# Half-size products for a third chunk of the first MLP matrix, with sums on GpSimd, finer waits and more filler matmuls

## The chip, the cores and the metric

The kernel runs on one core of a Trainium2 chip. The metric is the device time of one execution in microseconds (us). Three executions of the kernel before took 300.26, 300.62 and 301.41 us; the median is 300.62. The engines are TensorE (PE in the profile, with its weight loads as PEld), VectorE (DVE), ScalarE (ACT), GpSimd (POOL) and SyncE (SP).

## The reference

Eight batches, eight heads, 576 positions, head size 64. Attention looks back over a window of 128 positions with a linear bias per head; its output is laid side by side by heads to rows of 512, and goes through a normalisation, a two-layer MLP (512 to 2048 to 512) and a residual add.

```python
mask = (rel >= 0) & (rel < window)
scores = np.where(mask, scale * q @ k.T + slopes * -abs(rel), -1e9)
attn = softmax(scores)                      # by row
x = (attn @ v).transpose(0, 2, 1, 3).reshape(B, S, H * D)     # 8 x 576 x 512
xn = (x - mean) / sqrt(var + 1e-6) * g_ln
out = x + np.maximum(xn @ w_ch1, 0.0) @ w_ch2
```

## The kernel before

The 4608 rows are 36 blocks of 128. Blocks are gathered into 11 chunks: four of 2 blocks (chunks 0 to 3) and seven of 4 blocks (chunks 4 to 10). A program that ran before the kernel was written down has fixed the order of all work: the text `ORDER` (line 119) is a list of words `name:engine`, where `T` is TensorE (with the PSUM bank as a number), `V` VectorE, `A` ScalarE, `G` GpSimd and `S` SyncE. A word `~n` stands for n filler matmuls of 128x128 that compute nothing (`keep_warm`, L1287). Each engine runs its own words in the order of the list, and waits only for the data and buffers that a task needs. Tasks are declared with the engines they may run on and a planner's cost in us; the cost doesn't appear in the built program.

Per block: q and k come in by GpSimd DMA issues (L496) with a cast to f16, from block 9 on a SyncE DMA turns them (`QT`, L710, into `qkt`); before that TensorE does (`T`, L695). `S` multiplies k by q into the PSUM tiles `sc` (L732); ScalarE takes the exponential into `probs` (`exa`, `exb`, L780); from block 5 on VectorE multiplies `probs` by a table (`mka`, `mkb`, L787), of which there are three kinds: `mreg`, `mmix` and `mnew`. `pva` and `pvb` multiply by v (L808); VectorE normalises (`rc`, `nm`, L825 and L829) into `xb`, takes mean and variance (`bn`, `ag`), and writes `xs` (L892), which a SyncE DMA turns into `xt` (`XT`, L921).

Per chunk: the first MLP product is 16 tasks `A` of four matmuls 128x512 (L1210), each with a relu into `ht` (`r`, L1225 and L1227). The second product of chunks 0 to 3 is plain (`B`, L1247). From chunk 4 on it is made as seven half-size products instead of eight (`seven`, tasks `Pa` to `Pg`, L992), after the scheme of Strassen and Winograd: sums `sa` to `sd` of quarters of `ht` (two halves each, L982) and sums of the weights made once (`sumT`, L952), and reads of PSUM with adds (`ra` to `rg`, L1004).

In the last two chunks (`BOTH = 9`, chunks 9 and 10) the first product is made in the same way (`fours`): for each of four groups of outputs, seven products `Ua` to `Ug` of four matmuls 128x256 (L1121) with sums of the weights (`sumW`, made once in `first_sums`, L1079) and sums of `xt` (`tx`, L1098), copies of products out of PSUM (`ca`, `cb`, `cc`, L1132 and L1134), adds `ja` to `jc` (L1144) and relus (`rja` to `rjd`, L1149, L1151, L1180).

Sums lie in buffers that their owners no longer need: `sumW` in the three tables, `tx` in tiles of the `qkt` ring, the copies in tiles of the `probs` ring. Before the change all of them wait for the last mask product, and for the last reader of all tiles of `probs` and `qkt` (the list `free` in `first_sums`). All sums are VectorE's. The four PSUM banks `u` of the first product take the place of `sc` when the first `Ua` comes.

Of the kernel before, what the change touches and what calls it, by code (L numbers as in the profile page):

```python
# [119 lines left out]
dist:G qs0.0.i:S iden1:G ks0.0.i:S dist01:G dist00:G qs1.0.i:S iden2:G sid5:V sid3:V ks1.0.i:S sid2:V sid0:V sid1:V sid4:V sid7:V sid6:V v0.i:S  # L120
iden3:V ~38 Za0:T0 Zb0:T0 cT0.00:A g.i:A cT0.10:G w0.i:G ~16 T0.0:T0 cT0.01:A q2.i:G eT0.00:V cT0.11:V k2.i:G ~8 Sa0:T0 T0.1:T1 exa0:A v1.i:G eT0.01:A
eT0.10:V Za1:T0 cv0:A G:T2 q3.i:G eT0.11:A k3.i:G Sb0:T0 Gc:A Sa1:T0 exb0:A pva0:T0 v2.i:G Gk:T1 rc0.0:V exa1:A nm0.0:V Zb1:T0 w3.i:G pvb0:T2 Sb1:T0
rc1.0:V nm1.0:V v3.i:G exb1:A mu0:V xs0:V w1.i:G ~10 T2:T0 Z2:T0 w2.i:G ev2:V pvb1:T2 pva1:T3 q5.i:G rc1.1:V S2:T0 rc0.1:V nm1.1:V TX0:T0 exb2:A
nm0.1:V q4.i:G xt0:V exa2:A ~4 T3:T2 mu1:V k4.i:G xs1:V Z3:T0 ev3:A bn1:V w4.i:G TX1:T3 pva2:T0 pvb2:T2 xt1:V S3:T0 Gkc:V rc0.2:V w5.i:G rc1.2:V
A0.0:T3 nm0.2:V exb3:A nm1.2:V w6.i:G A0.12:T1 mu2:V exa3:A xs2:V A0.14:T0 bn0:V r0.12:A r0.0:V pvb3:T2 r0.14:A Z4:T0 rc1.3:V ag0:V pva3:T1 w7.i:G
nm1.3:V A0.2:T3 rc0.3:V nm0.3:V TX2:T0 mu3:V A0.6:T2 xs3:V xt2:A A0.4:T1 r0.6:V k5.i:G bn3:V TX3:T0 r0.4:A A0.8:T2 v4.i:G bn2:V xt3:A ag1:V A0.10:T1
ag2:V k6.i:G r0.8:A A1.14:T0 q6.i:G r0.10:V r0.2:V A1.12:T2 r1.14:A ln0:A T4:T1 rs0:A r1.12:A A1.0:T3 ev4:A q7.i:G A1.4:T0 B1.0:T2 r1.4:V r1.0:V
A1.6:T1 k8.i:G S4:T0 A1.10:T0 exa4:A r1.6:A B0.0:T3 r1.10:A k8.i:G exb4:A B1.4:T2 A1.2:T1 sumT0.0:V B0.4:T3 r1.2:V q8.i:G B1.8:T2 sumT0.1:V k7.i:G
sumT0.2:V B0.8:T3 q8.i:G sumT0.3:V B1.12:T2 q9.i:G T5:T0 o1.0:V B0.12:T3 ev5:A v5.i:G sumT1.0:V pvb4:T1 B2.0:T2 o0.0:V k9.i:G mreg30:A mreg10:A
rc1.4:V mreg11:A pva4:T0 nm1.4:V S5:T0 mreg01:A k10.i:G rc0.4:V nm0.4:V B3.0:T3 exb5:A sumT1.1:V v6.i:G T6:T1 mu4:V exa5:A ag3:V xs4:V q10.i:G A1.8:T0  # L130
ev6:V mreg20:A B3.4:T3 k11.i:G mreg31:A bn4:V mreg21:A ln1:A S6:T0 mreg00:A r1.8:V v7.i:G rs1:A T8:T1 mkb5:V exb6:A dist2:G T7:T0 ev8:V B3.8:T3
q11.i:G exa6:A mka5:V pvb5:T1 q12.i:G ev7:V B2.4:T2 rc1.5:V QT9.i:S nm1.5:V v8.i:G pva5:T0 B2.8:T2 rc0.5:V nm0.5:V k12.i:G mka6:V S7:T0 v8.i:G mu5:V
B2.12:T2 mkb6:V exb7:A QT10.i:S xs5:V v9.i:G TX4:T1 exa7:A B3.12:T3 xt4:V k13.i:G mmixc:V TX5:T0 pva6:T1 o3.0:V xt5:A S8:T0 q13.i:G o2.0:V pvb6:T0
exb8:A A2.2:T3 v11.i:G mkb7:V A2.8:T2 mnewc:V r2.2:A v10.i:G QT11.i:S z2:V mka7:V A2.0:T3 r2.8:A rc1.6:V rc0.6:V z1:V A2.14:T2 r2.0:A nm1.6:V mkb8:V
exa8:A A2.12:T0 nm0.6:V sumT1.2:V pvb7:T3 r2.12:A pva7:T1 bn5:V S9:T0 r2.14:A QT12.i:S rc1.7:V A2.4:T0 z3:V exb9:A ag4:V nm1.7:V A2.10:T2 mu6:V exa9:A
xs6:V A2.6:T3 k15.i:G rc0.7:V bn6:V XT6.i:S r2.4:A mka8:V S10:T0 q15.i:G r2.6:A nm0.7:V B5.0:T0 r2.10:A mu7:V exa10:A ag6:V xs7:V pvb8:T3 pva8:T1
B5.4:T0 ag5:V exb10:A bn7:V XT7.i:S k16.i:G rc1.8:V B4.0:T2 mka9:V k15.i:G nm1.8:V QT13.i:S S11:T0 rc0.8:V dist2a:G nm0.8:V q15.i:G B4.4:T2 mkb9:V
exb11:A v13.i:G bn8:V B5.8:T0 exa11:A mkb11:V q14.i:G pvb9:T3 pva9:T1 ln2:A mka11:V B4.8:T2 rs2:A k14.i:G ag8:V rc0.9:V rc1.9:V B5.12:T0 nm0.9:V
v12.i:G ag7:V nm1.9:V ln3:A B4.12:T2 rs3:A bn9:V k17.i:G mkb10:V pvb11:T1 A3.2:T3 q16.i:G ag9:V o4.0:V ln9:A rs9:A S12:T0 r3.2:A q17.i:G xs8:V
rc1.11:V pva11:T2 o5.0:V XT8.i:S exb12:A A3.0:T3 xs9:V exa12:A A3.4:T0 nm1.11:V XT9.i:S rc0.11:V mka10:V A3.8:T1 r3.4:A nm0.11:V bn11:V A3.6:T0 r3.8:A  # L140
mkb12:V r3.0:A pvb10:T2 pva10:T1 QT14.i:S rc1.10:V S13:T0 rc0.10:V nm0.10:V A3.10:T3 exa13:A nm1.10:V out1.0.i:S bn10:V pvb12:T1 out0.0.i:S r3.6:A
A3.14:T2 ag11:V r3.10:V B6.0:T0 ag10:V r3.14:V ln11:A rs11:A exb13:A A3.12:T3 xs10:V mka13:V XT10.i:S scaleW2:A B7.0:T2 xs11:V r3.12:V B6.4:T0
XT11.i:S scaleW3:V B7.4:T2 scaleW1:A QT15.i:S B6.8:T0 rc1.12:V mkb13:V nm1.12:V B7.8:T2 k19.i:G B6.12:T0 QT16.i:S scaleW0:A v15.i:G S14:T0 o6.0:V
v14.i:G pva13:T3 mka12:V B7.12:T2 out2.0.i:S rc0.13:V exa14:A nm0.13:V pvb13:T1 pva12:T0 o7.0:V A4.8:T3 v20.i:G exb14:A rc1.13:V rc0.12:V nm1.13:V
A4.1:T2 v16.i:G nm0.12:V QT17.i:S mkb14:V S15:T0 r4.1:A v15.i:G mka14:V A4.3:T1 exb15:A bn12:V q18.i:G A4.0:T0 sumT1.3:V exa15:A k18.i:G r4.8:V
A4.10:T2 mka15:V q21.i:G S16:T0 r4.10:A r4.3:V A4.12:T3 q19.i:G exb16:A r4.0:V A4.11:T2 bn13:V q20.i:G exa16:A ag12:V r4.12:V A4.4:T1 dist1:G r4.11:A
mkb15:V k20.i:G A4.9:T0 r4.4:A ag13:V mka16:V v17.i:G ln13:A pvb14:T3 rs13:A A4.15:T2 r4.9:A xs12:V rc1.14:V XT12.i:S nm1.14:V pva14:T1 pva15:T0
rc0.14:V A4.7:T3 nm0.14:V QT18.i:S rc0.15:V nm0.15:V A4.14:T1 r4.7:A xs13:V mkb16:V A4.2:T0 out3.0.i:S bn14:V pvb15:T3 r4.2:A S17:T0 r4.15:A sa4.0:V
A4.6:T0 r4.14:A rc1.15:V sb4.0:V exb17:A A4.5:T2 XT13.i:S nm1.15:V r4.6:A A4.13:T1 bn15:V out6.0.i:S r4.5:A ag14:V sc4.0:V Pa4.00:T3 r4.13:A Pb4.00:T0
QT19.i:S exa17:A sa4.1:V Pa4.01:T3 Pb4.01:T0 ag15:V ln15:A Pa4.10:T3 out5.0.i:S rs15:A Pb4.10:T0 xs14:V out4.0.i:S Pa4.11:T3 xs15:V XT14.i:S Pb4.11:T0  # L150
sb4.1:V pvb16:T2 ra4.0:V k23.i:G pva16:T1 S18:T0 XT15.i:S rb4.0:V k21.i:G Pc4.00:T3 exb18:A Pc4.10:T3 sd4.0:V Pd4.00:T0 v24.i:G rc1.16:V exa18:A
QT20.i:S mka17:V Pc4.11:T3 Pd4.01:T0 k22.i:G rc0.16:V nm1.16:V Pc4.01:T3 mkb17:V Pd4.10:T0 v19.i:G rc4.0:V pva17:T2 Pd4.11:T0 q22.i:G nm0.16:V S19:T0
rd4.0:V Pe4.00:T3 v18.i:G exb19:A sc4.1:V Pe4.10:T3 pvb17:T1 rc0.17:V dist1a:G Pf4.10:T0 q23.i:G rc1.17:V nm0.17:V Pf4.00:T0 sd4.1:V Pe4.11:T3 q24.i:G
Pe4.01:T3 nm1.17:V Pf4.11:T0 k22.i:G QT21.i:S Pf4.01:T0 A5.0:T2 q22.i:G rf4.0:V A5.9:T1 bn17:V v23.i:G r5.0:A re4.0:V exa19:A A5.7:T0 v22.i:G mkb19:V
Pg4.00:T3 q25.i:G r5.9:V S20:T0 bn16:V Pg4.10:T3 k24.i:G exa20:A mka19:V A5.2:T2 v21.i:G mkb18:V Pg4.11:T3 QT23.i:S r5.2:A r5.7:V Pg4.01:T3 k25.i:G
# [58 lines left out]
def kernel(  # L214
# [49 lines left out]
    HALVED = []  # L264
    SPANS = [0]
    SEVEN = 4
    BOTH = 9
    BEFORE = 28.0
    AHEAD = 1.2
    SUMS_V = 40.0  # L270
# [700 lines left out]
    def seven(c, relu, v0):  # L971
# [8 lines left out]
        def sums(name, h, out, in0, in1, op, deps, v):  # L980
            def emit(e, b):
                nc.vector.tensor_tensor(out=out, in0=in0, in1=in1, op=op)  # L982
# [347 lines left out]
```

## Time and profile before

| | |
|---|---|
| median of three executions | 300.62 us |
| the profiled execution | 300.98 us, span of the instructions 299.1 us |
| TensorE busy | 293.3 us, 3014 matmuls, mean granted clock 0.994 |
| VectorE busy | 242.8 us |
| ScalarE busy | 165.3 us |
| GpSimd busy | 105.4 us, DMA issues nearly all |
| first product of the first chunk starts | 19.6 us |
| last matmul starts | 295.6 us |

Matmuls are pipelined, and the profile models their ends, so a busy TensorE may still lose time between two starts. A wait of an engine is put down to the last thing that released it. GpSimd's DMA issues count as busy time of GpSimd.

### The profile page before, as it was taken

Reading aid. Unit: us, or ns where it says so; the run is one execution under the profiler, and the core shown is the slowest. Engines: PE = TensorE matmul, PEld = TensorE weight load, DVE = VectorE, ACT = ScalarE, POOL = GpSimd, SP = SyncE. Lnnn points to the kernel's source line nnn. Section 1 sums busy time; section 2 is a strip of 40 time slices with the busy share of each in tenths; the row PEclk is TensorE's granted clock in tenths of the full one; section 3 lists DMA queues with packets and bytes.
Section 4 is the critical chain, followed back from the end, with each engine's and each line's share of the span. In section 5 each row is a group of like instructions: output and inputs, shape, how many; then the busy total and the mean of one; then the engine's idle time right before and its main releaser. Section 6 shows DMA issues by size and latency. Waiting matters only on the chain.

```text
span 299.1 us, 7458 instructions
## 1 busy us (share of the span) xinstructions
PE 293.3 (98%) x3014; PEld 225.1 (75%) x3014; DVE 242.8 (81%) x583; ACT 165.3 (55%) x273; POOL 105.4 (35%) x138
## 2 busy tenths in 40 slices
PE   8999999999999999899999999999999999999995
PEld 8789756875955578566886588657787799999984
DVE  3397289998879879849978888788899988988983
ACT  3664536794798573368528444676544655245500
POOL 5965369738137428433633567300000000000000
PEclk9799999999999999999999999999999999999999
DMA  6999999999999999999999999968101033012015
GB/s 179 159 196 194 206 144 141 146 138 133 122 219 145 151 224 133 145 140 167 179 166 197 182 159 143 158 171 150 36 19 55 0 125 89 2 37 106 35 55 193
DMA packets 163779, 39.93 MB, mean 133 GB/s; under 512 B 154017, under 2 KB 159137, under 8 KB 163746
## 3 DMA queue, kind: packets, MB, share of 16 engines
q0 software_dynamic: 110000, 17.70, 95.6%
q1 hardware_dynamic: 53744, 21.77, 40.5%
q8 instruction: 23, 0.38, 0.6%
q14 instruction: 10, 0.08, 0.1%
q10 hardware_dynamic: 2, 0.00, 0.0%
HBM read 36.70 MB, written 9.44 MB: 154 GB/s over the span
## 4 chain that ended last, share of the span: by engine, by line
PE 94%; DMA 4%; DVE 1%; ACT 0%; issue 0%
PE fb L1210 32%; PE fb L992 27%; PE fb L1247 9%; PE u L1121 8%; PE sc L732 6%; PE fb L808 6%; DMA qkt<-qk 4%; PE fb L1287 2%; PE sc L748 1%; PE fb L695 1%; PE fb L440 0%; PE fb L906 0%; PE fb L426 0%; DVE ot L1004 0%; DVE xb L829 0%; ACT probs L780 0%
## 5 line engine op out<-in xcount | busy, mean ns | idle before, releaser
L1210 PE MATMUL fb<-xt,w1sb 128*128 128x512 f16 (+1 forms) x576 | 106.4, 332 | 0.6 <-DMA xt<-xs 0.6
L780 ACT ACTIVATE probs<-sc 128x1024 f16<-128x1024 f32 (+1 forms) x72 | 67.4, 975 | 36.0 <-PE sc L732 27.3
L1210 PEld LDWEIGHTS <-w1sb 128*128 128x128 f16 x576 | 61.5, 114 | 27.8 <-DMA xt<-xs 0.9
L1227 ACT ACTIVATE ht<-fb 128x512 f16<-128x512 f32 x88 | 51.1, 598 | 44.4 <-PE fb L1210 44.2
L992 PEld LDWEIGHTS <-ht 128*128 128x128 f16 x560 | 53.2, 98 | 9.2
L496 POOL DMA_DIRECT2D qk<-in_k_dram x38 | 32.8, 866 | 44.3 <-DMA qkt<-qk 36.8
L992 PE MATMUL fb<-w2sb,ht 128*128 128x256 f16 x336 | 44.7, 273 | 0.0
L496 POOL DMA_DIRECT2D qk<-in_q_dram x38 | 32.5, 861 | 16.6 <-DMA qkt<-qk 9.6
L496 POOL DMA_DIRECT2D vx<-in_v_dram x36 | 31.0, 868 | 15.6 <-PE fb L808 12.4
L787 DVE TENSOR_TENSOR probs<-probs,mreg 128x1024 f16<-128x1024 f16 (+1 forms) x46 | 30.4, 667 | 1.1 <-ACT probs L780 1.0
L992 PE MATMUL fb<-ks,ht 128*128 128x256 f16 x224 | 30.8, 273 | 0.0
L1247 PE MATMUL fb<-w2sb,ht 128*128 128x512 f16 x128 | 30.7, 379 | 0.0
L829 DVE SCALAR_TENSOR_TENSOR xb<-fb,rec 128x256 f16<-128x256 f32 x72 | 29.5, 416 | 0.9
L808 PEld LDWEIGHTS <-probs 128*128 128x128 f16 x544 | 23.9, 98 | 6.8
L808 PE MATMUL fb<-vx,probs 128*128 128x65 f16 x496 | 26.1, 194 | 0.0
L1004 DVE TENSOR_TENSOR ot<-fb,xb 128x512 f32<-128x512 f32 (+1 forms) x31 | 19.6, 634 | 6.0 <-PE fb L992 5.6
L848 DVE BATCH_NORM_STATS2 st<-xb 128x6 f32<-128x512 f16 x36 | 24.2, 682 | 0.2
L825 DVE RECIPROCAL rec<-fb 128x4 f32<-128x4 f32 x72 | 12.2, 174 | 14.7 <-PE fb L808 12.4
L1225 DVE TENSOR_SCALAR ht<-fb 128x512 f16<-128x512 f32 x24 | 16.0, 681 | 8.4 <-PE fb L1210 8.3
L1247 PEld LDWEIGHTS <-ht 128*128 128x128 f16 x128 | 11.6, 98 | 11.1
L732 PEld LDWEIGHTS <-qkt 64*128 64x128 f16 x496 | 14.9, 94 | 6.4 <-issue 5.3
L1144 DVE TENSOR_TENSOR ht<-u,probs 128x512 f16<-128x512 f32 x24 | 16.2, 685 | 2.7 <-PE u L1121 1.8
(113 smaller groups left out, 387.7 us busy)
## 6 DMA issues: line engine op xcount, KB each, us to landing
out_dram<-ot SPq DMA_DIRECT2D x32, 256.0 KB, 2.9
qk<-in_q_dram POOLq DMA_DIRECT2D x30, 128.0 KB, 7.6
qk<-in_k_dram POOLq DMA_DIRECT2D x30, 128.0 KB, 7.2
vx<-in_v_dram POOLq DMA_DIRECT2D x28, 128.0 KB, 7.7
w1sb<-in_moe_w_ch_dram POOLq DMA_DIRECT2D x4, 512.0 KB, 9.1
w2sb<-in_moe_w_ch_dram POOLq DMA_DIRECT2D x4, 512.0 KB, 14.1
out_dram<-ot SPq DMA_DIRECT2D x8, 128.0 KB, 1.8
qs<-in_q_dram SPq DMA_DIRECT2D x2, 256.0 KB, 3.6
```

The lines of the kernel that those rows point to most:

```text
L496: nc.gpsimd.dma_start(out=dst(p0, n), in_=src[b, :, s0 : s0 + n, :].rearrange("h p d -> p h d"))
L732: nc.tensor.matmul(scs[half][:, g, c0 : c0 + P], kt[rows, 1, hp, :], qkt[i][rows, 0, hp, :], start=not bias, stop=True, skip_group_check=True,
L780: nc.scalar.activation(out=o, in_=n_, func=AF.Exp, scale=inv_sqrt_d)
L787: en.tensor_tensor(out=pv, in0=pv, in1=mask[:, 2 * half : 2 * half + 2, :, lo:], op=ALU.mult)
L808: nc.tensor.matmul(pp[:, hh * (D + 1) : hh * (D + 1) + D + 1], probs[i][:, bank, slot, side * P : side * P + P], vx[i if side else before] ...
L829: nc.vector.scalar_tensor_tensor(out=xb[c][:, j, 256 * half : 256 * half + 256].rearrange("p (h d) -> p h d", d=D), in0=pp[:, :, 0:D], sca ...
L848: nc.vector.bn_stats(out=st[i][:, :], in_=xb[c][:, j, :])
L992: nc.tensor.matmul(o, lhs(f, p), rhs(f), start=first and f == 0 and (p == 0 or key[0] != key[1]), stop=f == F2 - 1, skip_group_check=True)
L1121: nc.tensor.matmul(late[bank][:, FOURTH * f : FOURTH * f + FOURTH], w, rhs[kb], start=first and f == kb == 0, stop=kb == 1, skip_group_che ...
L1210: nc.tensor.matmul(fb[b][:, n_ * x : n_ * x + n_], w1f[f // CB][:, kb, (f + x) % CB, :], xt[c][:, kb, 0:n_], start=(kb == x == 0), stop=(k ...
L1227: nc.scalar.activation(out=o, in_=src, func=AF.Relu)
L1247: nc.tensor.matmul(pm[:, 0 : c1 - c0], ht[c][:, f, j * P : j * P + P], w2sb[f // CB][:, f % CB, c0:c1], start=(f == 0), stop=(f == NFB - 1),)
```

## The change

1. `BOTH` goes from 9 to 8: chunk 8's first product is made with seven half-size products for each of four groups, too.
2. The sums that lie in SBUF alone (`sa` to `sd`, `sumW`, `tx`) may run on GpSimd. In the new order 31 of the 56 `sa` to `sd`, all 8 `sumW` and 8 of now 12 `tx` do.
3. The waits are finer: a `sumW` waits for the masks that use its table alone, a `tx` for the readers of its tile of `qkt`, a copy for the readers of its tile of `probs`, and the first `Ua` for the exponentials, whose PSUM banks it takes. The three `sumW` buffers are dealt to the tables in another order.
4. The whole list `ORDER` is new. Its opening has fillers `~38 ~23 ~15 ~6 ~6 ~7` where it had `~38 ~16 ~8 ~10 ~4`; some tasks of the opening have changed engines, the loads of weights and of q, k and v stand in another order, and so do the transposes on SyncE.

Pieces of the order after the change, the first from the opening, the second from chunk 8 and 9:

```
sid4:V ~38 Za0:T0 cT0.00:A Zb0:T0 g.i:A cT0.10:G w0.i:G ~23 T0.0:T0 cT0.01:V q2.i:G eT0.00:A cT0.11:V k2.i:G eT0.01:V ~15 Sa0:T0 T0.1:T1 exa0:A v1.i:G
eT0.10:V ~6 Za1:T0 eT0.11:V Sb0:T0 cv0:G G:T2 exb0:A q3.i:G k3.i:G Zb1:T0 Gc:V pva0:T0 Sa1:T0 rc0.0:V v2.i:G pvb0:T1 nm0.0:V Sb1:T0 exa1:A rc1.0:V
...
sa8.0:G rjc8.2:A Ug8.3:T0 Uc9.0:T0 jc8.3:V rjd8.3:A Ud9.0:T0 bn35:V cb9.0:A Ua9.1:T0 ra8.0:V Pb8.01:T3 ca9.1:A sb8.0:G Ub9.1:T0 cc9.0:V rjc8.3:A
Pb8.10:T3 rjb8.2:A ja9.1:V Ue9.0:T0 rja9.0:A Uc9.1:T0 sa8.1:V Pb8.11:T3 ln33:A Ud9.1:T0 sb8.1:G rb8.0:V Pc8.00:T0 cc9.1:A Uf9.0:T0 ag35:V jb9.0:V
```

```diff
-    BOTH = 9
+    BOTH = 8
...
-    wsum = [[t[:, 2 * m : 2 * m + 2, :, :].rearrange("p a s c -> p (a s c)").rearrange("p (k f) -> p k f", k=2) for m in range(2)] for t in (mreg, mmix, mnew)]
+    wsum = [[t[:, 2 * m : 2 * m + 2, :, :].rearrange("p a s c -> p (a s c)").rearrange("p (k f) -> p k f", k=2) for m in range(2)] for t in (mmix, mnew, mreg)]
...
-            masked.append(pr[-1])
+            masked[kind].append(pr[-1])
...
         def sums(name, h, out, in0, in1, op, deps, v):
             def emit(e, b):
-                nc.vector.tensor_tensor(out=out, in0=in0, in1=in1, op=op)
-            return add(f"{name}{c}.{h}", ("DVE", 0.69), emit, deps, v)
+                (nc.vector if e == "DVE" else nc.gpsimd).tensor_tensor(out=out, in0=in0, in1=in1, op=op)
+            return add(f"{name}{c}.{h}", Choice("DVE", {"DVE": 0.69, "POOL": 2.25}), emit, deps, v)
...
-        free = [t for r_ in (probs, qkt) for ts_ in r_.readers.values() for t in ts_] + masked
-        wsums["free"] = free
...
-                    nc.vector.tensor_tensor(out=dst, in0=x, in1=y, op=op)
-                need = prev[-1:] + scaled[m :: 2] + free
-                if n == 2:
-                    need = need + plain_all[m + 2]
-                prev.append(add(f"sumW{m}.{n}", ("DVE", 0.72), emit, need, FIRST[BOTH] / CB * SPAN - BEFORE - 12.0 + n))
+                    (nc.vector if e == "DVE" else nc.gpsimd).tensor_tensor(out=dst, in0=x, in1=y, op=op)
+                need = prev[-1:] + scaled[m :: 2] + (plain_all[m + 2] if n == 2 else masked[(1, 2, 0, 0)[n]])
+                prev.append(add(f"sumW{m}.{n}", Choice("DVE", {"DVE": 0.72, "POOL": 2.25}), emit, need, FIRST[BOTH] / CB * SPAN - BEFORE - 12.0 + n))
...
+    def tile_reads(ring_, n):
+        return [t for k, ts in ring_.readers.items() if k not in ring_.pins and ring_.turn(k) % len(ring_.tiles) == n for t in ts]
...
-                nc.vector.tensor_tensor(out=dst, in0=x, in1=y, op=ALU.subtract)
-            t = add(f"tx{c}.{n}", ("DVE", 0.42), emit, done + prev[1:2] + prev[0:1] + x_use[c % 2] + masked, v0 - 6.0 + n)
+                (nc.vector if e == "DVE" else nc.gpsimd).tensor_tensor(out=dst, in0=x, in1=y, op=ALU.subtract)
+            was = tile_reads(qkt, 2 * (c % 2) + n // 2)
+            t = add(f"tx{c}.{n}", Choice("DVE", {"DVE": 0.42, "POOL": 1.2}), emit, done + prev[1:2] + prev[0:1] + x_use[c % 2] + was, v0 - 6.0 + n)
...
-            p1 = product("Ua", 0, xbank, plain_w(0, 0), plain_x(0, 0), True, done + sc_ + wsums["free"])
-            c1 = copy("ca", 0, xbank, cps[0], [p1] + old[0:1])
+            p1 = product("Ua", 0, xbank, plain_w(0, 0), plain_x(0, 0), True, done + sc_ + exps)
+            c1 = copy("ca", 0, xbank, cps[0], [p1] + old[0:1] + tile_reads(probs, 0))
```

## The prediction

> **What bounds the kernel now.** I read the page's busy line first, then the times of PE by stretch, then what PE waited for.
>
> ```profile
> PE 293.3 (98%) x3014; PEld 225.1 (75%) x3014; DVE 242.8 (81%) x583; ACT 165.3 (55%) x273; POOL 105.4 (35%) x138
> PEclk9799999999999999999999999999999999999999
> ```
>
> ```profile
> 7.70:11.10 3.40, 3.30 (x32) 1.97 (x31) 0.90 (x3) 3.15 (x7) 3.40 (x5) 1.00 1.35 173
> 11.10:14.50 3.40, 3.40 (x32) 2.85 (x32) 1.58 (x7) 1.77 (x2) 2.87 (x4) 0.50 2.43 156
> ...
> 178.00:230.00 52.00, 52.00 (x553) 37.23 (x552) 44.76 (x108) 29.51 (x48) 9.75 (x12) 1.00 0.94 109
> 230.00:296.00 66.00, 65.91 (x583) 59.59 (x580) 58.07 (x114) 28.17 (x54) 0.00 (x0) 1.00 0.20 66
> ```
>
> ```profile
> PE fb L1287 <- DVE warm_t L387: 1.1, 1, 1.1
> PE fb L1210 <- DMA xt<-xs: 0.6, 1, 0.6
> PE sc L732 <- DMA qkt<-qk: 0.5, 1, 0.5
> PE fb L1287 <- DVE xb L829: 0.3, 1, 0.3
> ```
>
> TensorE is never without work for longer than 0.7 us between 19.7 and 296 us (columns of the second fence: stretch, length, busy PE, PEld, DVE, ACT, POOL, then clock and DMA). So a change gains what it takes out of PE's list, and loses what it makes PE wait. VectorE is 86 to 88% busy in the last two stretches; GpSimd has nothing after 195 us.
>
> The second thing to see is what happens where VectorE and GpSimd meet. The trace has no GpSimd sum, but a few neighbours:
>
> ```profile
> 48.54 0.69 DVE L703 COPY qkt<-fb 128x1024 f16<-128x1024 f16 x1 [0.15 <-PE fb L695]
> ...
> 48.86 0.46 POOL L416 COPY dist_t<-dist_t 128x256 f16<-128x256 f16 x1
> 49.14 0.73 DVE L787 TENSOR_TENSOR probs<-probs,mreg 128x1024 f16<-128x1024 f16 x1
> ```
>
> ```profile
> L787 DVE TENSOR_TENSOR probs<-probs,mreg x46: 416/681/729, 47.7 to 222.6; 128x1024 f16<-128x1024 f16 x44, 128x512 f16<-128x512 f16 x2
> L787 DVE TENSOR_TENSOR probs<-probs,mmix x8: 660/680/693, 58.8 to 202.5; 128x1024 f16<-128x1024 f16 x8
> ```
>
> ```profile
> L892 DVE TENSOR_SCALAR xs<-xb,mv,rstd x28: 382/406/564, 74.2 to 250.2; 128x512 f16<-128x512 f16 x28
> ```
>
> The one mask product that starts while a GpSimd copy reads SBUF is the longest of all, 729 ns; the timelines show no other of its size over 693. The `xs` rows that overlap a GpSimd DMA issue average 461 ns (8 of them), the other 20 average 403. The two keep each other waiting.
>
> **The change, part by part.** Sums are against the profiled execution: 300.98 us, span 299.1, 1.9 us outside it; the median of the runs is 300.62, 0.36 lower.
>
> Chunk 8's products. Before: 16 products of 4 matmuls 128x512; the chain has 8 of them in 1.73 us, so 64 x 216 ns = 13.82 us. After: 4 x 7 half products of 4 matmuls 128x256; the chain has 16 of L1121 in 1.75 us, so 112 x 109 ns = 12.23. Gain 1.59 us, all on the path. It adds 12 copies (599 ns, L1134) to ScalarE, 12 joins (685 ns, L1144) to VectorE, and as many relus as it takes away. ScalarE has 29.5 of 52 us in that stretch, and the same pattern in chunks 9 and 10 leaves PE 65.91 busy of 66, so I cost them at nothing; they cost PE up to 0.6 us a product if ScalarE falls behind. The finer waits let `Ua8` start before the last masks are done; no time by itself.
>
> The opening. Fillers go from 76 to 95. Sixteen take 1.06 us and eight 0.61, so 56 ns each: 1.05 us more, and the idle PE time between 4.3 and 19.7 us in which they could lie is 0.46. That is 0.6 us lost, if nothing else moves. But the clock of 0.50 for 3.40 us costs 1.70 us of PE's work, it follows the stretch in which weight loads are rarest (1.97 of 3.40 us), and 44 of the 95 fillers (before, 24 of 76) now stand just ahead of or in it. I take the clock as granted: -1.1; ends -1.7 and +0.6.
>
> Transfers. Two waits at 120.6 and 124.5 us cost PE 1.42 us (start to start, less the rows' own 109 ns); the second is for a transpose that landed 10.6 us after its issue. The order of all loads and transposes is new, so these waits can go, stay, or be replaced: I take half, -0.7; ends -1.4 and 0.
>
> So without GpSimd the sum is 300.98 - 1.59 - 1.1 - 0.7 = 297.6.
>
> The sums on GpSimd. 31 of the 56 `s` sums, all 8 `sumW` and 8 of 12 `tx` move. VectorE loses 39 x 0.68 + 4 x 0.41 and gains 8.2 of joins: 20 us less, on an engine that is not the bound, so no gain. Price of one on GpSimd: the one-input rows are 0.46 to 0.48 us for 256 columns (L415, L416) and 0.76 for 512 (L629), so 1.14 ns a column and 0.18 us at the start; 1.34 us for 1024 columns if the second input is free, 2.51 if it costs as much as the first. VectorE's rows say that a second input counts (TENSOR_TENSOR 414 ns against TENSOR_SCALAR 284 at 512 columns), so I go near the upper end: 2.2 us, and 1.15 for a `tx`. The Trainium skill (GPSIMD Engine Reference, section 3.1) has 4,497 ns for a two-input add of 2,048 fp32 columns; an estimate by it is 2.25 us for half as many, which no row here shows, and the sum would be 1 us higher.
>
> Where they stand decides. From the word `sumW1.0:G` to `sd8.1:G` PE has 8 A products, 88 half products, 4 S and 13 pv: 8 x 0.864 + 88 x 0.436 + 4 x 0.63 + 13 x 0.24 = 50.9 us. GpSimd has 17 sums, 7 `tx` and 2 load issues: 17 x 2.2 + 7 x 1.15 + 2 x 0.87 = 47.2. It is 93% full with no wait at all, and PE consumes each sum soon: `sa8.0` and `sb8.0` (4.4 us) have 11 half products (4.8 us) until `Pc8.00`. In the same stretch VectorE still has 9 masks, 7 sums, a `tx`, 9 `xs` and 4 relus from SBUF: 16 x 0.68 + 0.41 + 9 x 0.40 + 4 x 0.28 = 16.0 us. If the two exclude each other, their work adds up: 45.5 + 16.0 = 61.5 against 50.9 (the load issues leave VectorE free), and PE waits 10.6 us. Ends: 0 with the low price (28.1 + 16.0 fits), 17.2 with the high one (52.1 + 16.0). If they don't meet: 0, or 2.9 with the high price (52.1 + 1.7).
>
> Of the two other stretches, `sc4.0` to `sd6.0` (PE 68.2 us) has 12 sums and 34 load issues, 26.4 + 29.6 = 56 us on GpSimd, and `sa9.0` to `sd10.0` (PE 32.3 us) 10 sums and a `tx`, 23.2, beside 7 on VectorE. Both fit added up, but each sum can come late by a mask or sum of 0.68 us; I take 2 us for both, ends 0 and 5. Behind a waiting sum on GpSimd stand the loads of q, k and v, 47 of them up to `sumW1.0`; S waits for those.
>
> The mask's row is what I go by: 49 ns more in a meeting of 173 ns, of which the first 85 lie under the instruction before it (it ends at 49.23), so more than half of what remained. That is nearer to exclusion than to none. The Trainium skill (SBUF — State Buffer, section Who interferes with whom) says that a VectorE instruction with two SBUF inputs and a GpSimd instruction that reads SBUF block each other fully, for whichever started first, to its end. The trace agrees that they meet, but its one meeting is too short to show the full block; by the page the sum is 310, and without it 298.
>
> **Forecast:** 297.6 + 10.6 + 2 = 310.2 us.
>
> **The rivals.** (1) They hardly meet, and GpSimd keeps up: 297.6, faster; ends 296.3 (clock and waits all gained) and 300.0. It decides at a full price, waits included, of 2.38 us a sum (20.5 x 2.38 + 2.1 = 50.9). For it: 34 masks beside GpSimd's DMA issues average 678 ns against 679 without. Against it: the 729 ns, and a margin of 7%. (2) They share: half of VectorE's 16.0 us falls on GpSimd, 47.2 + 8 - 50.9 = 4.3, so 301.9 (299.5 to 305). (3) No contention, but loads held up behind waiting sums make S late twice, 1.4 us each as at 120 us: 300.4. For it: GpSimd already waits 46 us for free buffers; against it: loads run several blocks ahead.
>
> **How the numbers follow.** Forecast 0.51, rivals 0.33, 0.11 and 0.05. A change under 0.5% (1.5 us of 300.62: 299.1 to 302.1) can't be told from none. Faster: 0.30 of (1) and 0.03 of (2), 0.33. Same: 0.03 + 0.04 + 0.05 and 0.01 of the forecast's low end, 0.13. Slower: 0.54. The likeliest case alone runs from 302 (a price of 1.9 us: 39.3 + 16.0 - 50.9 = 4.4) to 300.0 + 17.2 + 5 = 322, all terms at their upper ends. The range is 296.9 to 322.0: it reaches down into (1) and leaves out only the part of it where clock and waits are both gained whole.
>
> **What would show it.** Right: mask products and `xs` of VectorE well over 0.69 and 0.41 us wherever a GpSimd sum runs; GpSimd nearly 100% busy from about 180 to 235 us; PE waiting there, for GpSimd or for joins and reads of a late VectorE. A clock of 1.00 at 11 to 14.5 us and no wait near 120 us show the small terms. Wrong: VectorE's rows unchanged beside sums of 2.2 us or less, and PE without gaps.

## The result, and the profile after

The changed kernel takes 329.14 us (median of 6 runs, 325.31 to 330.72), the kernel before 300.76 in the same session: 1.092 times as long, interval 1.086 to 1.098. The forecast was 310.2, range 296.9 to 322.0. The profiled execution took 330.72 us, span 329.0; all rows below are from it. It is the longest of the six, over 1.5% above the fastest, and counts as a slow run; without it the median is 329.05. The sign is as forecast, and VectorE and GpSimd do hold each other up; but the loss is three times the size, and most of what is beyond the forecast lies in a stretch for which the prediction had almost nothing.

The busy line and the granted clock on the page of the changed kernel:

```profile
PE 302.8 (92%) x3081; PEld 234.3 (71%) x3081; DVE 270.6 (82%) x561; ACT 165.4 (50%) x275; POOL 203.0 (62%) x186
PEclk9999999999999998998799989999899999999999
```

PE idles 26.2 us of the span (5.8 before). Its busy time went up by 9.5 us although it has less to multiply. The stretches (stretch, length, busy PE, PEld, DVE, ACT, POOL, clock, DMA) show where:

```profile
7.70:11.10 3.40, 3.40 (x45) 2.83 (x43) 1.23 (x4) 1.36 (x3) 3.40 (x5) 1.00 1.36 171
11.10:14.50 3.40, 3.40 (x40) 2.26 (x40) 2.38 (x9) 1.95 (x3) 3.40 (x5) 1.00 2.46 156
107.00:200.00 93.00, 82.04 (x806) 57.78 (x805) 80.31 (x141) 38.35 (x59) 63.14 (x59) 0.93 1.35 134
...
153.60:160.40 6.80, 6.08 (x52) 4.54 (x52) 5.86 (x12) 1.94 (x2) 5.80 (x6) 0.50 1.29 191
213.00:282.00 69.00, 59.40 (x594) 49.63 (x592) 66.53 (x113) 36.50 (x67) 49.51 (x26) 0.98 0.32 62
282.00:326.00 44.00, 43.69 (x399) 40.41 (x397) 31.08 (x51) 19.53 (x35) 22.90 (x13) 1.00 0.21 69
```

The half clock of the opening is gone (1.00 from 11.1 to 14.5 us). `sc4.0` to `sd6.0` lie in the row from 107 us, `sumW1.0` to `sd8.1` in the one from 213, the last 11 sums in the one from 282. PE idles 11.0 us in the first, 9.6 in the second, 0.3 in the third. The clock halves four times, in or right behind such idle times: at 122.9, 153.6 (twice as long), 194.6 and 228.7 us, 17.1 us in all, which costs 8.5 us of PE's work. How long it is halved differs between executions: the fastest has a mean clock of 0.989 against 0.974 here, that is 3.6 us of work lost (0.011 of its span of 323.6 us), and it is 5.4 us shorter.

What PE waits for (the chain of waits, PE alone):

```profile
PE fb L996 <- DVE ot L1008: 7.1, 6, 2.3
PE fb L1214 <- DVE xb L833: 6.3, 3, 2.3
PE fb L812 <- DVE xb L833: 5.5, 3, 4.2
PE fb L996 <- DVE xb L833: 1.1, 1, 1.1
...
PE fb L1214 <- DMA xt<-xs: 0.8, 1, 0.8
```

All the large ones are for VectorE, and for its reads of PSUM (L1008, L833), which are no longer than in the kernel before (at most 692 and 425 ns). GpSimd is not in the list. The timeline shows the link:

```profile
116.12 2.12 POOL L986 TENSOR_TENSOR ht<-ht 128x1024 f16<-128x1024 f16 x1
...
116.75 2.04 DVE L791 TENSOR_TENSOR probs<-probs,mreg 128x1024 f16<-128x1024 f16 x1
...
118.72 2.48 DVE L896 TENSOR_SCALAR xs<-xb,mv,rstd 128x512 f16<-128x512 f16 x1
...
118.91 2.13 POOL L986 TENSOR_TENSOR ht<-ht,ks 128x1024 f16<-128x1024 f16 x1
...
121.12 0.68 DVE L1008 TENSOR_TENSOR ot<-fb,xb 128x512 f32<-128x512 f32 x1
...
121.85 0.60 PE L996 MATMUL fb<-ks,ht 128*128 128x256 f16 x4 [2.13 <-DVE ot L1008]
```

A mask (0.68 us elsewhere) starts while a sum runs and ends at 118.8, after the sum has ended at 118.2. The `xs` behind it (0.40 us elsewhere) meets the next sum and ends at 121.2, after that one's 121.0. The read `ot` stands third in VectorE's queue, and PE's bank comes free 2.1 us late. One microsecond later the clock halves.

The rows of the operations themselves, over the whole run (min, median, max in ns):

```profile
L791 DVE TENSOR_TENSOR probs<-probs,mreg x46: 414/682/2615, 46.2 to 252.3; 128x1024 f16<-128x1024 f16 x44, 128x512 f16<-128x512 f16 x2
L896 DVE TENSOR_SCALAR xs<-xb,mv,rstd x28: 375/410/2480, 75.3 to 281.7; 128x512 f16<-128x512 f16 x28
...
L833 DVE SCALAR_TENSOR_TENSOR xb<-fb,rec x72: 352/415/425, 12.9 to 272.5; 128x256 f16<-128x256 f32 x72
```

```profile
L986 POOL TENSOR_TENSOR ht<-ht x8: 2107/2131/2561, 109.5 to 313.2; 128x1024 f16<-128x1024 f16 x8
```

The maxima of masks and `xs` went from 729 and 564 ns to 2615 (3241 for a mask on `mnew`) and 2480; the read of PSUM at L833 has not moved. A sum on GpSimd takes 2.13 us, up to 2.6 when it was the one that waited. Added up, VectorE's rows are longer than usual for their shape by 20.0 us in the stretch from 107 us (12 rows, as many as there are sums), 18.6 from 213 (15 rows), and 3.0 from 282.

**A ledger of PE's lost time.** Count each useful matmul that has begun by a time t at the usual start-to-start of its shape in the kernel before (216 ns for 512 columns, 109 for 256, 56 for 128, 32 for a pv, 29 for an S, 109 to 527 for the 18 of f32; fillers at nothing). t less that sum is what PE has lost by t. The useful work is 278.1 us before and 276.5 in every kernel below. Differences to the kernel before, in us, from one profiled execution each:

| | work | to 19.7 | to 100 | 100 to 200 | 200 to 290 | end | span |
|---|---|---|---|---|---|---|---|
| predicted | -1.6 | -1.1 | 0 | +1.3 | +10.6 | 0 | +9.2 |
| changed kernel | -1.6 | +0.5 | +1.0 | +16.6 | +13.1 | +0.3 | +29.9 |
| all sums on VectorE (1) | -1.6 | +0.3 | +0.5 | +0.6 | +5.6 | +1.8 | +7.2 |
| the same and spare sums (2) | -1.6 | +0.9 | +2.2 | +16.5 | +41.5 | +3.5 | +62.9 |
| the same and fills (3) | -1.6 | +0.2 | +1.4 | +1.9 | +9.4 | +0.5 | +11.7 |
| first 12 and last 11 on GpSimd (5) | -1.6 | +0.6 | +2.1 | +16.0 | +5.5 | +0.3 | +22.9 |
| middle 24 on GpSimd (6) | -1.6 | -0.2 | +1.8 | +1.2 | +12.6 | +0.6 | +14.4 |
| all 47 cut thin (7) | -1.6 | +0.2 | +0.8 | +0.5 | -0.2 | 0 | -0.3 |
| last 11 on GpSimd (8) | -1.6 | +0.6 | +1.4 | +0.1 | +5.2 | 0 | +5.7 |
| all 47 in pieces (9) | -1.6 | +0.3 | +1.9 | +2.6 | +12.1 | 0 | +15.3 |
| last 11, the middle 24 cut thin (12) | -1.6 | +0.3 | +1.3 | +1.3 | 0.0 | -0.1 | +1.2 |

(The numbers in brackets are those of the experiments below. For the prediction, the two DMA waits and the 2 us of "the two other stretches" are put at 100 to 200.)

### The profile page after: what moved, and what is told of

Its sections match the earlier page's. It is cut to its first block, busy times and chain, and to the rows that moved or that the text cites. A ratio compares the mean times of both kernels' runs of the same rounds, so it can differ in the third digit from the quotient of the medians.

```text
span 329.0 us, 7683 instructions
## 1 busy us (share of the span) xinstructions
PE 302.8 (92%) x3081; PEld 234.3 (71%) x3081; DVE 270.6 (82%) x561; ACT 165.4 (50%) x275; POOL 203.0 (62%) x186
## 4 chain that ended last, share of the span: by engine, by line
PE 43%; DVE 17%; issue 3%; ACT 0%
PE fb L996 22%; PE u L1125 10%; PE fb L1214 8%; DVE probs L791 5%; DVE xs L896 4%; PE fb L812 2%; PE sc L735 2%; DVE ks L986 2%; DVE ot L1008 2%; DVE xb L833 1%; DVE qs L986 1%; DVE ht L1148 1%; DVE st L852 1%; DVE ht L1229 1%; DVE ht L986 0%
## 5 line engine op out<-in xcount | busy, mean ns | idle before, releaser
L1214 PE MATMUL fb<-xt,w1sb 128*128 128x256 f16 (+1 forms) x512 | 90.6, 327 | 7.1 <-DVE xb L833 6.3
L1214 PEld LDWEIGHTS <-w1sb 128*128 128x128 f16 x512 | 54.9, 114 | 31.0 <-issue 8.4
L996 PEld LDWEIGHTS <-ht 128*128 128x128 f16 x560 | 54.3, 100 | 14.0 <-issue 5.0
L1231 ACT ACTIVATE ht<-fb 128x512 f16<-128x512 f32 x70 | 40.7, 598 | 39.8 <-PE fb L1214 37.4
L791 DVE TENSOR_TENSOR probs<-probs,mreg 128x1024 f16<-128x1024 f16 (+1 forms) x46 | 40.6, 890 | 0.9 <-ACT probs L783 0.8
L833 DVE SCALAR_TENSOR_TENSOR xb<-fb,rec 128x256 f16<-128x256 f32 x72 | 29.0, 413 | 0.9
L986 POOL TENSOR_TENSOR qs<-ht 128x1024 f16<-128x1024 f16 x6 | 12.8, 2132 | 25.3 <-DVE ht L1229 10.9
L1008 DVE TENSOR_TENSOR ot<-fb,xb 128x512 f32<-128x512 f32 (+1 forms) x31 | 19.3, 630 | 10.5 <-PE fb L996 10.5
L896 DVE TENSOR_SCALAR xs<-xb,mv,rstd 128x512 f16<-128x512 f16 x28 | 26.0, 933 | 1.6 <-ACT rstd L889 1.6
L986 POOL TENSOR_TENSOR ht<-ht,ks 128x1024 f16<-128x1024 f16 x10 | 22.6, 2266 | 7.3 <-ACT probs L1138 5.3
L1148 DVE TENSOR_TENSOR ht<-u,probs 128x512 f16<-128x512 f32 x36 | 23.6, 681 | 3.1 <-PE u L1125 2.9
L1138 ACT ACTIVATE probs<-u 128x512 f32<-128x512 f32 x33 | 19.0, 596 | 10.7 <-PE u L1125 10.6
```

What stands on the lines that cost most here:

```text
L791: en.tensor_tensor(out=pv, in0=pv, in1=mask[:, 2 * half : 2 * half + 2, :, lo:], op=ALU.mult)
L833: nc.vector.scalar_tensor_tensor(out=xb[c][:, j, 256 * half : 256 * half + 256].rearrange("p (h d) -> p h d", d=D), in0=pp[:, :, 0:D], sca ...
L896: nc.vector.tensor_scalar(out=xs[x][:, :], in0=xb[c][:, y, :], scalar1=mv[c][:, y, 0:1], scalar2=rstd[c][:, y : y + 1], op0=ALU.subtract, ...
L986: (nc.vector if e == "DVE" else nc.gpsimd).tensor_tensor(out=out, in0=in0, in1=in1, op=op)
L996: nc.tensor.matmul(o, lhs(f, p), rhs(f), start=first and f == 0 and (p == 0 or key[0] != key[1]), stop=f == F2 - 1, skip_group_check=True)
L1214: nc.tensor.matmul(fb[b][:, n_ * x : n_ * x + n_], w1f[f // CB][:, kb, (f + x) % CB, :], xt[c][:, kb, 0:n_], start=(kb == x == 0), stop=(k ...
```

## The experiments

In all of them a `before` of the same session stands at 300.4 to 300.9 us.

**1. All sums back on VectorE.** `:G` becomes `:V` for the 47 words in ORDER, as in

```
-A4.14:T2 sb4.0:V sc4.0:G r4.12:A
+A4.14:T2 sb4.0:V sc4.0:V r4.12:A
...
```

> All 47 sums that stand on GpSimd in the changed kernel go back to VectorE, at the same places in the order; everything else of the change stays. Theory (VectorE and GpSimd hold each other up, and that is the whole loss): VectorE's masks are back at 0.68 us and xs at 0.40, PE waits under 2 us in all, and the time is 297 to 301. Rival one (the sums' results come late, because GpSimd is too slow or too full): the same time, so it is not told apart here. Rival two (the new order of the loads, the finer waits or chunk 8's half products cost the time): PE still waits 10 us or more, and the time is 310 or above.

Measured: 309.04 us, ratio 1.0285 (1.0249 to 1.0322). Masks are back (the longest of the 46 on `mreg` is 694 ns):

```profile
L791 DVE TENSOR_TENSOR probs<-probs,mreg x46: 414/680/694, 46.2 to 225.7; 128x1024 f16<-128x1024 f16 x44, 128x512 f16<-128x512 f16 x2
```

So 20 of the 28.4 us come of having the sums on GpSimd. But 8 us remain, and neither my 297 to 301 nor the rival's 310 has them. The ledger puts 5.6 of them at 200 to 290 us.

**2. Sums that nobody reads.** As experiment 1, with a spare sum on GpSimd at each of the 47 places.

```
-sc4.0:G
+sc4.0:V dus:G
+nc.gpsimd.tensor_tensor(out=spare[:, 0:n], in0=spare[:, 0:n], in1=spare[:, 0:n], op=ALU.add)
```

> The sums are on VectorE as in the run before this one, and GpSimd has, at the places where it had them, sums of the same size (39 of 128x1024, 8 of 128x512) on a spare tile, whose results nobody reads. This is extra work that the reference does not need. Theory (holding up): VectorE's masks and xs that meet a sum take 1 to 3 us again, and since VectorE now also has the real sums, the time is 315 to 340. Rival one (late results): nothing waits for these sums, so the time is within 2 us of the run without them, but for loads that come late behind them.

Measured: 360.41 us, 1.198 (1.193 to 1.203), 51 us above experiment 1 and 20 over my upper end. VectorE has the real sums and the waits for the spare ones:

```profile
L791 DVE TENSOR_TENSOR probs<-probs,mreg x46: 417/682/3316, 47.1 to 281.9; 128x1024 f16<-128x1024 f16 x44, 128x512 f16<-128x512 f16 x2
L896 DVE TENSOR_SCALAR xs<-xb,mv,rstd x28: 376/408/3394, 75.5 to 313.5; 128x512 f16<-128x512 f16 x28
```

Nobody waits for a result here, so late results are not needed for the loss: holding VectorE up is enough. By the ledger it costs 16.5 us from 100 to 200 us, the same as in the changed kernel, and 41.5 from 200 to 290, where the changed kernel, whose VectorE is rid of the real sums, loses 13.1.

**3. Fills in place of the spare sums.**

```
-nc.gpsimd.tensor_tensor(out=spare[:, 0:n], in0=spare[:, 0:n], in1=spare[:, 0:n], op=ALU.add)
+[nc.gpsimd.memset(spare[:, 0:n], 0.0) for _ in range(2)]
```

> As the run before this one, but each spare sum is two fills of the same spare tile (one for a small one), which write SBUF and read nothing; a fill of 128x128 took 0.2 us in the changed kernel, so two of 128x1024 are about 1.5 to 2 us. If a GpSimd instruction holds VectorE only because it reads SBUF: masks stay at 0.68 us, and the time is within 2 us of the run with the sums on VectorE alone. If any GpSimd instruction holds it: masks of 1 us and more, and 310 to 335.

Measured: 313.06 us, 1.043 (1.039 to 1.048), 4.0 above experiment 1 and between my two cases, with 83.5 us of fills on GpSimd (91.7 us of sums in experiment 2; the small ones are two fills, too). Masks keep their time, but not `xs`:

```profile
L791 DVE TENSOR_TENSOR probs<-probs,mreg x46: 416/678/692, 46.2 to 229.5; 128x1024 f16<-128x1024 f16 x44, 128x512 f16<-128x512 f16 x2
L896 DVE TENSOR_SCALAR xs<-xb,mv,rstd x28: 377/410/1601, 74.7 to 263.5; 128x512 f16<-128x512 f16 x28
```

So it is GpSimd's reading that holds a mask, while the scaling of one f16 tile is held by a fill as well. GpSimd, which also issues the loads of q, k and v, is nearly as full here, and PE waits 0.4 us in all for a transfer: that loads come late is not the cause either.

**4. The meetings by themselves.** A small kernel: eight forms of VectorE alone, then eight of each in a row beside GpSimd sums, one-input copies and fills that run without a pause.

```
"mask": lambda: nc.vector.tensor_tensor(out=vo[:, :], in0=va[:, :], in1=vb[:, :], op=ALU.mult),
"scale": lambda: nc.vector.tensor_scalar(out=vo[:, 0:512], in0=va[:, 0:512], scalar1=sc[:, 0:1], scalar2=sc[:, 1:2], op0=ALU.subtract, op1=ALU.mult),
...
"join": lambda: nc.vector.tensor_tensor(out=vo[:, 0:512], in0=ps[:, :], in1=fa[:, :], op=ALU.add),
...
"sum": lambda: nc.gpsimd.tensor_tensor(out=go[:, :], in0=ga[:, :], in1=gb[:, :], op=ALU.add),
```

> A kernel that leaves out the whole computation: it writes zeros, and lets VectorE run eight forms of instruction, each six times alone and eight times beside GpSimd, which runs 128x1024 sums (2.1 us), one-input copies or fills without a pause. Theory: masks (two SBUF inputs) take 0.68 us alone and about 2.1 to 2.8 us each beside sums, one to one in turn; the scaling with two columns and the relu (one SBUF input, f16) are held up as the xs of the changed kernel are (up to 2.5 us); statistics, the join and the read from PSUM keep their times within 5%. Beside one-input copies the same, with shorter waits. Beside fills no form changes, if reading is what holds. The rival that they share the port: every form of VectorE slows by the same ratio, and no single one by more than 2x.

The timeline has each row of eight (six alone) in one line, start and length in us:

```profile
4.06 4.30 DVE L44 TENSOR_TENSOR vo<-va,vb 128x1024 f16<-128x1024 f16 x6
8.40 2.66 DVE L45 TENSOR_SCALAR vo<-va,sc 128x512 f16<-128x512 f16 x6
...
50.58 20.23 DVE L44 TENSOR_TENSOR vo<-va,vb 128x1024 f16<-128x1024 f16 x8 [17.86 <-POOL va L75]
...
75.05 15.69 DVE L45 TENSOR_SCALAR vo<-va,sc 128x512 f16<-128x512 f16 x8
...
141.58 5.77 DVE L48 TENSOR_TENSOR vo<-pt,fa 128x512 f16<-128x512 f32 x8
```

Length by number, in us:

| VectorE | alone | beside sums | copies | fills |
|---|---|---|---|---|
| mask, 2 SBUF inputs f16 | 0.72 | 2.53 | 1.45 | 0.72 |
| sum of two f32 tiles, 512 | 0.72 | 2.29 | 1.35 | 0.75 |
| scale, 1 input f16, 512 | 0.44 | 1.96 | 1.01 | 1.04 |
| relu, 1 input f16, 512 | 0.32 | 1.95 | 0.99 | 1.04 |
| copy, 1 input f16, 1024 | 0.45 | 2.03 | 1.08 | 1.17 |
| statistics, 512 | 0.72 | 0.73 | 0.73 | 0.73 |
| join, PSUM and SBUF | 0.72 | 0.72 | 0.72 | 0.72 |
| read of PSUM | 0.72 | 0.72 | 0.72 | 0.75 |

Eight masks and sums take turns one to one. Beside fills scale, relu and copy get longer, which I had not expected. The Trainium skill (SBUF — State Buffer, section Who interferes with whom) names the same two groups (two SBUF inputs, only against a GpSimd instruction that reads; one input in a fast mode, against any), with a full block for the whole instruction. The table agrees with it in all eight rows. Sharing, by the same ratio for all, falls.

**5 and 6. The middle 24 sums on VectorE, or they alone on GpSimd.** The engine letters of the 24 words from `sumW1.0` to `sd8.1`, or of the other 23.

```
-sumW1.0:G
+sumW1.0:V
...
-sd8.1:G
+sd8.1:V
```

> The 24 sums from sumW1.0 to sd8.1, where the prediction put 10.6 of the 12.6 us, go back to VectorE; the 12 before (sc4.0 to sd6.0) and the 11 behind stay on GpSimd. By the prediction's terms the two other stretches cost 2 us: 311, 2 above the 309.0 with all sums on VectorE. By the trace of the changed kernel (VectorE's rows are 20.0 us too long in the stretch of the first 12 sums, and PE loses about as much): 322 to 330.

> The opposite: only the 24 sums from sumW1.0 to sd8.1 are on GpSimd, the 12 before and the 11 behind are on VectorE. By the prediction: 309.0 + 10.6 = 320. By the trace of the changed kernel, where PE loses 13.5 us in that stretch and VectorE gets 24 sums off a stretch in which it was 97% busy: 314 to 320. If the losses of the two stretches simply add up, this run and the one before it lie above 309.0 by 20 us together, no more, no less; if one slow stretch hides the other's loss, by more.

Measured: 320.06 us (three runs, 318.71 to 322.14; the profiled one took 323.68), 1.064 (1.059 to 1.070), with the middle on VectorE; 315.52, 1.049 (1.044 to 1.055), with only the middle on GpSimd. The first is 11.0 above experiment 1, the second 6.5, 17.5 together against 20.1 with both. The first lies 2 us below the trace's estimate and 9 above the prediction's; the second lies within the trace's estimate and 4.5 below the prediction's. VectorE's rows are too long by about 19.5 us between 107 and 200 us in the first and by 15.9 between 200 and 260 in the second. The 12 early sums cost more than the 24 that I had priced.

**7. Thin sums.** The 47 sums stay on GpSimd, with 4 of each 256 or 512 columns.

```
-nc.gpsimd.tensor_tensor(out=out, in0=in0, in1=in1, op=op)
+nc.gpsimd.tensor_tensor(out=out[:, :, 0:4], in0=in0[:, :, 0:4], in1=in1[:, :, 0:4], op=op)
```

> The changed kernel with each of its 47 GpSimd sums cut to 16 or 8 of its 1024 or 512 columns, so that they cost almost nothing and stand on GpSimd as before; chunks 4 to 10 are then computed from sums that are mostly left out (and one tile is filled once, in the stretch before, so that nothing is read that was never written). The prediction's sum without GpSimd: 297.6. If VectorE's load with the sums back (97% busy from 180 to 230 us) is what makes 309.0 of it, and the new order costs its opening and its end: 300 to 304. If the new order itself is slow somewhere else: 306 or above.

Measured: 301.00 us, 1.001 (0.998 to 1.004). Free sums bring the kernel back to where it was, no further. The rest of the change is worth nothing in time, where I had 297.6: in the ledger the 1.6 us less of work are given back but for 0.3, 0.8 of them between 19.7 and 100 us.

**8. Only the last 11 sums on GpSimd.**

```
-sc4.0:G
+sc4.0:V
...
-sd8.1:G
+sd8.1:V
```

> Only the 11 sums from sa9.0 on stay on GpSimd, behind the last mask and the last xs; the 36 before are on VectorE. Theory (what costs time is a meeting with masks and xs): nothing is lost, 307 to 310, the same as with all sums on VectorE. Rival (a sum on GpSimd takes three times as long, and PE waits for it): 11 times about 1 us more, 315 or above.

Measured: 307.36 us, 1.022 (1.017 to 1.028). Eleven sums of up to 2.1 us lose nothing where VectorE has no mask and no `xs` left. From 200 to 260 us, ahead of them, PE is not full and VectorE nearly is (57.56 of 60 us):

```profile
200.00:260.00 60.00, 56.67 (x578) 49.09 (x577) 57.56 (x131) 34.88 (x64) 0.00 (x0) 1.00 0.29 65
```

**9. Four pieces.** All 47 sums on GpSimd, each in pieces of 256 columns.

```
+for k_ in range(out.shape[1]):
+    for w_ in range(0, out.shape[2], 256):
+        p_ = (slice(None), k_, slice(w_, w_ + 256))
+        nc.gpsimd.tensor_tensor(out=out[p_], in0=in0[p_], in1=in1[p_], op=op)
```

> The changed kernel, all 47 sums on GpSimd, but each 128x1024 sum is made of four instructions of 128x256 and each 128x512 of two. GpSimd's own work grows: from the rows of 1157 ns at 512 and 2132 ns at 1024 columns, 0.18 us at the start and 1.9 ns a column, so about 0.67 us a piece and 2.7 us a sum. Theory (VectorE is held for the length of the one instruction that GpSimd has running): no mask is held for more than about 0.7 us, 1.4 in all, VectorE's rows are 10 to 18 us too long instead of 41.6, and the time falls to 306 to 315. Rival (sums come late because GpSimd is too slow): they come 25% later, and the time is 329 to 340.

Measured: 316.14 us, 1.050 (1.047 to 1.054), 13 less than the changed kernel, though GpSimd is busy 25.7 us longer. So the length of the one instruction sets much of the price, but not everywhere: in the ledger the stretch from 100 to 200 us falls from 16.6 to 2.6, the one from 200 to 290 only from 13.1 to 12.1. The time is 1 us above my range, and VectorE's rows are still too long by 11 us between 107 and 200 us and 14 between 200 and 282, more than the 10 to 18 that I had for all. The timeline shows that a mask's wait is not bounded by one piece:

```profile
109.15 3.95 POOL L992 TENSOR_TENSOR ht<-ht 128x256 f16<-128x256 f16 x4 [1.79 <-DVE qs L987]
109.71 1.16 DVE L791 TENSOR_TENSOR probs<-probs,mnew 128x1024 f16<-128x1024 f16 x1
...
223.94 1.30 POOL L1119 TENSOR_TENSOR qkt<-xt 128x256 f16<-128x256 f16 x2
224.37 4.55 DVE L791 TENSOR_TENSOR probs<-probs,mreg 128x1024 f16<-128x1024 f16 x1
...
225.20 2.53 POOL L992 TENSOR_TENSOR ht<-ht,ks 128x256 f16<-128x256 f16 x4
...
227.70 2.36 POOL L1119 TENSOR_TENSOR qkt<-xt,qkt 128x256 f16<-128x256 f16 x3
```

At 109 us they take turns. At 224 the row of one mask is 4.55 us long (0.68 elsewhere): it starts while a piece runs, and six more pieces, the last at 227.70, go ahead of it.

**10. The old fillers.** 76 as before, in the kernel of experiment 8.

```
-w0.i:G ~23 T0.0:T0
+w0.i:G ~16 T0.0:T0
...
-eT0.01:V ~15 Sa0:T0
+eT0.01:V ~8 Sa0:T0
...
-eT0.10:V ~6 Za1:T0
+eT0.10:V Za1:T0
...
-v3.i:G ~6 T2:T0
+v3.i:G ~10 T2:T0
...
-exa2:A ~7 T3:T2
+exa2:A ~4 T3:T2
```

> The 76 fillers of the kernel before, in the counts that they had there (38, 16, 8, none, 10, 4), in the order of the changed kernel with the last 11 sums on GpSimd (307.4 with 95 fillers). By the prediction: 1.05 us of fillers less, but the half clock at 11 to 14.5 us comes back and costs 1.7, so 308.0. Rival (the fillers buy no clock): the clock stays 1.00 there, and 306.3. Rival two (they fill gaps and change nothing): 307.4.

Measured: 309.60 us, 1.028 (1.025 to 1.031), against 1.022 (1.017 to 1.028) with 95: the intervals overlap, so the time alone does not settle it. The clock does:

```profile
11.10:14.50 3.40, 3.40 (x42) 2.94 (x42) 2.83 (x9) 1.94 (x2) 3.40 (x5) 0.83 2.42 156
14.50:19.70 5.20, 4.80 (x70) 4.46 (x67) 3.10 (x11) 1.57 (x3) 4.70 (x7) 0.78 1.74 187
```

3.4 us at half clock are back (17% of 3.4 and 22% of 5.2 us are 1.7 us of work). The fillers buy the clock that the prediction said. By 19.7 us this kernel has lost 0.7 us more in the ledger than that of experiment 8 (1.3 against 0.6), as the prediction's 1.70 less 1.05 has it. The rest of the difference lies between 100 and 200 us (1.9 against 0.1); why is open.

**11. Relus to ScalarE.** In the kernel of experiment 8, 21 relus and copies from chunk 4 on.

```
-r4.11:V
+r4.11:A
...
-rja8.2:V
+rja8.2:A
...
-cc9.0:V
+cc9.0:A
```

> From chunk 4 on, 21 relus and copies of 0.28 to 0.69 us go from VectorE to ScalarE, which is about half busy there; the sums are on VectorE but for the last 11. Theory (what is left of the loss, 6.6 us above the kernel before, is VectorE being full from about 190 to 260 us): up to 12 us less on VectorE, and 303 to 306. Rival (the order of the rest is at fault): 307 or above.

Measured: 307.39 us, 1.022 (1.018 to 1.026): nothing gained, against my theory. VectorE lost 11.3 us of work, but 9.3 of it before 200 us, and only 1.0 from 200 to 260, where PE is busy 56.88 of 60 us (56.67 in experiment 8). Between 107 and 200 us PE is busy 2.3 us less than there (90.25 against 92.59), so ScalarE's longer queue may have cost what was gained; it does not settle the theory.

**12. The middle 24 thin, on VectorE.** In the kernel of experiment 8.

```
-def emit(e, b):
+def emit(e, b, w_=4 if f"{name}{c}.{h}" in MID else None):
-    nc.vector.tensor_tensor(out=out, in0=in0, in1=in1, op=op)
+    nc.vector.tensor_tensor(out=out[:, :, 0:w_], in0=in0[:, :, 0:w_], in1=in1[:, :, 0:w_], op=op)
```

> The order with the last 11 sums on GpSimd and 36 on VectorE (307.4), where the 24 sums from sumW1.0 to sd8.1 stay on VectorE at their places but are cut to 4 of each 256 or 512 columns, which leaves most of the computation of those sums out. If these 24 sums on VectorE (13 us of its time in a stretch of 65 us in which it was full) are what is left of the loss: 300 to 302.5, as with all sums thin. If the 12 before or the 11 behind carry a part of it: 303.5 or above. If the order of the rest of that stretch is at fault: 306 to 308.

Measured: 302.42 us, 1.0075 (1.0039 to 1.011).

```profile
200.00:260.00 60.00, 60.00 (x629) 53.65 (x626) 51.75 (x135) 38.24 (x69) 2.87 (x2) 1.00 0.28 67
```

The time lies just inside the first case. PE is full again. The 24 sums cost 5 us on VectorE too, at these places in its order. With experiment 11 it stays open whether that is VectorE's load or where the sums stand in its queue; the places were not tried. No kernel beat the one before.

## Why the prediction was right or wrong

**What bounds the kernel**: right. The losses show as waits of PE and as a half clock behind them.

**Chunk 8's products, -1.59**: right as work, 278.1 to 276.5 us in the ledger. "I cost them at nothing" (the copies and joins) holds with free sums: nothing is lost from 200 to 290 us. With real sums on VectorE 5.2 to 5.6 us are lost there, which the prediction did not have.

**The opening, -1.1**: the mechanism is right (experiment 10), the net is not. The half clock went, 1.7 us. But by 19.7 us the kernels of the ledger have mostly lost 0.2 to 0.6 us more than the kernel before, up to 0.9 (experiment 2); one execution of the same opening (experiment 6) lost 0.2 less. In the changed kernel the first S starts at 9.0 us instead of 7.2, which I did not price. The term lies at its end of +0.6 more than at -1.1.

**Two DMA waits, -0.7**: right in size. One of 0.8 us is left, at another place (75 us), 1.42 before; that half would be left was a choice between the ends.

**Without GpSimd, 297.6**: 301.0 measured. The ledger has +0.2 in the opening, +0.8 up to 100 us and +0.5 up to 200, where I had -1.1, 0 and -0.7.

**The price of a sum, 2.2 and 1.15**: right; 2.13 and 1.16 alone, up to 2.6 and 1.6 when held. The Trainium skill's figure (GPSIMD Engine Reference, section 3.1), an estimate of 2.25 us by halving, agrees within 6%.

**`sumW1.0` to `sd8.1`, +10.6**: near in size, 13.1 us in the ledger from 200 to 290 (PE idles 9.6 us from 213 to 282, and the half clock takes 1.7), but partly by luck. My sum has GpSimd as the bound, "nearly 100% busy"; it was busy 49.5 of 69 us, and PE waited not for its results but for VectorE's reads. And with the sums on VectorE 5.6 of the 13.1 us remain; moving these 24 alone costs 6.5 (experiment 6).

**The two other stretches, +2 (ends 0 and 5)**: this step failed. "Both fit added up, but each sum can come late by a mask or sum of 0.68 us." The last stretch cost 0.3. The first cost 16.6 in the profiled execution: 11.0 of idle time and 6.8 of half clock, less 1.1 that was idle before. Of the 20.7 us between the predicted and the measured row of the ledger, 15.3 are in this column. That the 12 sums on GpSimd are the cause is shown: on VectorE they leave 0.1 to 0.6 us there (experiments 8 and 1), alone with the last 11 they cost 16.0 (5), unread ones 16.5 (2), pieces 2.6 (9). I added the work up on GpSimd, which had room, and asked how late its results come. What came late was VectorE: it has 12 sums to meet, 12 of its masks, `xs` and own sums were held, and 20.0 us of waiting fell on an engine that is busy 76.7 of these 93 us in the kernel before. Being in order, it passed them to the reads of PSUM behind, and PE got about half of them at once as idle time, though VectorE had 16 us to spare in the whole stretch. Twelve meetings at up to 2.1 us are a term of 0 to 25 us, and its ends were 0 and 5.

**What was not priced at all**: the clock behind PE's waits. Half clock followed four of them; 17.1 us of it here, 3.4 before, are 6.8 us more of PE's work, in this execution.

**The rivals**: (1) and (2) fall by the fourth experiment: forms that meet block each other wholly. (3) falls: PE's waits for loads are 0.8 us in all.

## What to carry to other kernels

Before work goes to GpSimd, list what VectorE runs beside it by form, and make the sum on VectorE's side as well: each of its instructions with two SBUF inputs, or in a fast one-input f16 form, can be held for the whole GpSimd instruction, and everything behind it in order with it. Moving was free where VectorE had no mask and no `xs` left and a quarter of its time to spare, as in the last stretch here; elsewhere shorter GpSimd instructions cut the price (329 to 316 us) but do not bound a single wait. An idle TensorE is paid for twice when its clock falls behind the gap.

## What the runs showed of the hardware that was not expected

- Fills on GpSimd, which read nothing, hold VectorE's scaling, relu and copy of one f16 tile (0.44 to 1.04 us, 0.32 to 1.04, 0.45 to 1.17), and no mask.
- Taking turns is not the rule: sums of 1024 columns alternated with masks one to one, while six pieces of 256 columns that started behind one mask went ahead of it (its row is 4.55 us long).
- The half clock came in pieces of 3.4 us, or twice that (153.6 to 160.4 us); in the changed kernel each began within, or at most 1.1 us behind, a start of a matmul that had been 2.4 to 4.4 us in coming. Two gaps of 2.5 and 2.3 us, ending at 219.1 and 222.9 us, were not followed by one until a third ended at 228.2.
